# Lead of the attention: three score tiles, merged exponentials, last keys by quarters, and an order that knows of tiling changes

## The chip, the cores and the metric

The kernel runs on one core of one Trainium2 chip. The metric is the device time of one execution in microseconds (us). The kernel before takes 1019.68 us, the median of three runs (1018.27 to 1021.52).

## The reference

Three blocks follow each other, all in float32, on 4 batches, 12 heads, 448 positions and heads of 64. B, S and DM below are 4, 448 and 768.

```python
# attention with a soft cap
scores = matmul(q, k.T) / sqrt(64)
scores = cap * tanh(scores / cap)
attn = exp(scores - max(scores)); attn = attn / (sum(attn) + 1e-9)
x = matmul(attn, v)                      # B, H, S, 64 -> x: B, S, DM = 12 * 64
# normalised FFN with a residual
xn = (x - mean(x)) / sqrt(var(x) + 1e-6) * g_ln
x = x + relu(xn @ w_ch1) @ w_ch2         # DM -> 4 DM -> DM
# gated MLP over positions
h = relu(x @ w_in); u, v = h[:512], h[512:]
v = (v - mean(v)) / sqrt(var(v) + 1e-6)
out = (u * (w_spatial @ v + b_spatial)) @ w_out
```

## The kernel before

**Layout.** Features stand on the 128 partitions and the 448 positions in the free dimension. Two heads are worked on together: they fill 64 partitions each, so that a product of one head takes half of the TensorE array and the other head's product runs beside it. The code calls the first head of such a pair `i`; this document calls the pair a unit. Batches 0 and 1 make units 0, 2, ... 22, batches 2 and 3 make 24 to 46. Attention products of the first two batches are float32, each of which the trace shows as two instructions; FFN products are float32 values split into a high and a low part of type float32r, three products for one.

**A unit of attention.** The 448 keys are three chunks of 128 and a last one of 64. `emit_s` computes the scores of a chunk transposed (keys on partitions) into a two-bank PSUM tile (`twos`, there are two), one bank a head: array shape 64 rows x 128 columns. ScalarE then applies Tanh (`expo`, from PSUM into an `es` tile) and Exp in place. The max isn't subtracted, since the cap bounds the scores. `emit_st` computes the last 64 keys of two units at once, with 64x64 quarters of the array, into two single banks; ScalarE works on each bank by itself (`hs` tiles). `emit_v` makes the products with the values (128 rows x 64 columns, two heads side by side). For the last keys it contracts over all 128 partitions, and half of the value tile is zero (memset at the start). VectorE adds up the three chunks' exponentials and then the last keys' (`add`, 64 partitions a head); a product with ones turns that into the sums over keys (128x32 for two units, 128x64 where a unit is `alone`: the last four heads of a batch). Reciprocals come back through DRAM (`invert`) or, for unit 22, from VectorE; `emit_n` multiplies and `x_done` adds the result to the sum over features from which the mean of a batch is made (`ln_mean`, `feature_sum`: two float32r products with ones). `ln_center` subtracts the mean and splits the result into `xn`.

**Stages.** `main` builds the program in this order: the lead (`attend` for units 0 to 22, with `ln_mean` and `ln_center` of batch 0 at place 16.2 of 24 and those of batch 1 after the last unit, and four FFN weight tiles through `make` from place 1.0 on), then `h_units`, the first FFN product of batches 0 and 1 (a unit of it is 18 products of 128x128, 3 for each of 6 feature blocks), with the attention of batches 2 and 3 between, and then second FFN products (`y_seven`), the gated MLP and a second pass for batches 2 and 3.

**The order.** Nothing above is the order on the chip. `Program` records every operation with a cost; `edges` finds what depends on what, `order` gives each a due time from the sum of TensorE costs before it, and `plan` plays the engines and at each step takes, on a free engine, the ready operation that is due first and for which buffers are free (`pick`, `room`). On TensorE a `group` is taken as one, with an added constant (`switch`) where the writer expected a change of array shape. TensorE may run ahead of its due times by 28 us (`AHEAD`). `Stage` opens a set of SBUF buffers when an earlier set has been used up. Operations in `either` go to VectorE or ScalarE, whichever plays out better.

Of the kernel before, what the change touches and what calls it, by code (L numbers as in the profile page):

```python
# [38 lines left out]
ST = 0.12  # L39

# [3 lines left out]
FIRST = 2, 7, 2, 10, 2, 2  # L44


AHEAD = 28
SLACK = 0.35
# [66 lines left out]
class Stage:  # L115


    def __init__(self, prog, tc, name, after=(), side=None):
        self.side = side
        self.tc, self.name, self.after, self.then, self.pools = tc, name, after, [], []  # L120
        self.open = not after
        self.left = 0
        self.pool = None
        for a in after:
            a.then.append(self)
        prog.stages.append(self)

    def begin(self):
        self.pool = self.tc.tile_pool(name=self.name, bufs=1, side=self.side)
        pool = self.pool.__enter__()  # L130
        for p in self.pools:
            for t in p.tiles:
                t.tile = pool.tile(t.shape, t.dt, name=t.name)
# [12 lines left out]
class Slots:  # L146


    def __init__(self, name, tiles, proto=None, stage=None):
        self.name, self.size = name, len(tiles)  # L150
# [65 lines left out]
class Program:  # L216
# [6 lines left out]
    def __init__(self, nc):  # L223
# [3 lines left out]
        self.at = {}  # L227
        self.stages = []
# [16 lines left out]
    def add(self, engine, cost, latency, call, writes, reads):  # L245
        o = self.open
        if o is None:
# [13 lines left out]
    def group(self, switch=0.0):  # L261


        self.switch = switch
# [3 lines left out]
        o[0][0][1] += self.switch  # L268
# [85 lines left out]
    def plan(self, due):  # L354
# [38 lines left out]

        def pick(e):

# [3 lines left out]
            found = None  # L399
            while q and found is None:  # L400
                d, i, k = heapq.heappop(q)
                if taken[i]:
                    continue
                if d > reach():
# [12 lines left out]
                if not room(i):  # L417
                    skipped.append((d, i, k))
                    continue
                found = i, k  # L420
            for x in skipped:
                heapq.heappush(q, x)
# [6 lines left out]
        while True:  # L429
            for e in ready:  # L430
# [13 lines left out]
                if e == "PE":  # L444
                    spent += cost
                free[e] = now + cost
# [24 lines left out]
            else:  # L471
                for b in bufs[x]:
                    b.left -= 1
                    if not b.left:
                        b.pool.give(b)
                        if b.pool.stage is not None and not b.pool.stage.left:
                            for s in b.pool.stage.then:
                                if not s.open and all(not a.left for a in s.after):
                                    s.open = True
                                    out.append((s, None))  # L480
                                    for p in s.pools:
                                        p.changes += 1
# [16 lines left out]
class Recorder:  # L499
# [3 lines left out]
    def __getattr__(self, method):  # L503
# [5 lines left out]
        def record(*args, **kw):  # L509
# [30 lines left out]
            self.program.add(self.name, cost, latency, call, [out], ins)  # L540
# [5 lines left out]
def attn_ffn_gmlp_kernel(  # L546
# [37 lines left out]
    def slots(name, n, shape, dt, pool=const):  # L584
# [6 lines left out]
            ("wh", [128, 2, DM], F32R), ("small", [128, 80], F32)), COUNTS))  # L591

    shapes = {"rb": ([128, 2, DH], F32R), "w6": ([128, DM, 2], I32), "es": ([128, 2, S], F32),
# [5 lines left out]
    def staged(stage, kind, n, name=None):  # L599
# [5 lines left out]
    mid = Stage(prog, tc, "mid", (one,))  # L605
# [6 lines left out]
    w6, es, qks, hx, wc, w4 = (  # L612
        staged(one, kind, n, name) for (kind, name), n in zip(
            (("w6", "w6"), ("es", "es"), ("qk", "qk"), ("acc", "hx"), ("wq", "wc"), ("w4", "w4")), FIRST))
# [16 lines left out]
    ones64 = const.tile([128, 64], F32, name="ones64")  # L631
    ones32 = const.tile([128, 2], F32, name="ones32")
    onesr = const.tile([128, 128], F32R, name="onesr")
# [3 lines left out]
    mhalf = const.tile([128, 64], F32, name="mhalf")  # L637
# [3 lines left out]
    banks = slots("bank", 4, [128, 512], F32, psum)  # L641
    twos = slots("two", 2, [128, 2, 512], F32, psum)

    def f(t):
        return t.bitcast(F32)

# [47 lines left out]
    def value(kind, j, home=None, pool=wr):  # L694
# [8 lines left out]
        else:  # L703
# [5 lines left out]
            if home is None:  # L709
                A.activation(out=t, in_=hi.bitcast(F32), func=ACTF.Prelu, scale=REBASE, alpha=-(2.0 ** 32))  # L710
            else:
                with prog.either():
                    for e in (V, A):
                        if e is A:
                            A.activation(out=t, in_=hi.bitcast(F32), func=ACTF.Copy, scale=REBASE)
                        else:
                            V.tensor_scalar(out=t, in0=hi.bitcast(F32), scalar1=REBASE, scalar2=None, op0=ALU.mult)
# [4 lines left out]
            else:  # L722
                V.tensor_scalar(out=ti, in0=ti, scalar1=3, scalar2=None, op0=ALU.logical_shift_left)
                if home is not None:
# [1086 lines left out]
```

## Time and profile before

| | us |
|---|---|
| median of 3 runs | 1019.68 (1018.27 to 1021.52) |
| span of the profiled execution | 1016.5 |
| busy: PE | 1002.0 (99%) |
| busy: VectorE (DVE) | 856.2 (84%) |
| busy: ScalarE (ACT) | 565.4 (56%) |
| chain that ended last | PE 75%, DMA 14%, DVE 5%, ACT 4% |

The profile page gives one execution by its span, from the first to the last instruction; it shows no other time of that execution, and the times of the runs are measured separately. Ends of matmuls are modelled, so a busy PE may still be waiting inside; the distance between the starts of its instructions tells more. All operations are recorded through one helper, so every row names the same line (L538); the tiles' names tell the operations apart: `two<-qk` are scores, `bank<-qk` last scores, `bank<-es,vt` and `bank<-hs,vt` values and last values, `bank<-es,ones` the sums, `bank<-rs,wh` and `bank<-rs,rs` FFN products, `bank<-wh,onesr` products of `feature_sum`.

### The profile page before, as it was taken

The numbers are of one execution on the slowest core, as the hardware profiler recorded it, in microseconds if no ns is written. First come the engines' busy times: TensorE is split into PE (matmuls) and PEld (weight loads), VectorE is DVE, ScalarE is ACT, GpSimd is POOL, SyncE is SP. The second block draws the span as 40 slices with busy tenths as digits, with TensorE's granted clock in tenths as the row PEclk, the third lists the DMA queues.
The fourth block names the chain that finished last, engine by engine and source line by source line (L and its number), as shares of the span: only waits on it lengthen the run. The fifth ranks groups of instructions, "written<-read, shape, count | busy, mean of one in ns | idle before, by whom it ended". The sixth has DMA issues, their size and how long they took to land.

```text
span 1016.5 us, 14927 instructions
## 1 busy us (share of the span) xinstructions
PE 1002.0 (99%) x5056; PEld 825.9 (81%) x5056; DVE 856.2 (84%) x1476; ACT 565.4 (56%) x897; POOL 24.3 (2%) x21
## 2 busy tenths in 40 slices
PE   7999999999999999999999999999999999999998
PEld 2332787787778889999889899999999999998887
DVE  6989998878888779989889989877788777778986
ACT  7999776776667344545566245544465322214553
POOL 0000110000000000000001110000000000000000
PEclk9999999999999999999999999999999999999999
DMA  8454779999999999999684233565799986602402
GB/s 261 154 139 144 256 279 360 359 337 369 338 370 363 358 341 403 409 329 375 244 259 144 50 133 117 165 203 194 236 336 395 337 267 222 192 21 71 132 17 109
DMA packets 132048, 248.71 MB, mean 245 GB/s; under 512 B 21970, under 2 KB 93828, under 8 KB 131972
## 3 DMA queue, kind: packets, MB, share of 16 engines
q1 hardware_dynamic: 131972, 247.76, 70.9%
q8 instruction: 40, 0.66, 0.3%
q14 instruction: 36, 0.29, 0.1%
HBM read 167.70 MB, written 80.01 MB: 244 GB/s over the span
## 4 chain that ended last, share of the span: by engine, by line
PE 75%; DMA 14%; DVE 5%; ACT 4%; issue 1%; SPq 1%; DVEq 0%; ACTq 0%
PE bank L538 50%; PE two L538 25%; DMA w<-in_w_dram 5%; DMA kept_w<-wc 3%; DMA hs<-inv 2%; ACT es L538 2%; DMA qk<-in_qk_dram 1%; DMA h<-hx 1%; ACT hs L538 1%; DVE x L538 1%; DMA inv<-rc 1%; SPq L538 1%; DVE rs L538 1%; DVE wh L538 1%; DVE small L538 1%
## 5 line engine op out<-in xcount | busy, mean ns | idle before, releaser
L538 PE MATMUL bank<-rs,wh 128*128 128x448 f32 x1704 | 357.1, 363 | 2.5 <-ACT hs L538 2.2
L538 PEld LDWEIGHTS bank<-rs,wh 128*128 128x128 f32 x1704 | 318.2, 187 | 29.9 <-ACT hs L538 4.4
L538 DVE TENSOR_TENSOR rs<-hs,rs 128x448 fp32r<-128x448 f32 x159 | 94.8, 619 | 3.7 <-ACT rs L538 3.1
L538 PE MATMUL two<-rs,wh 128*128 128x448 f32 x414 | 92.7, 362 | 0.0
L538 ACT ACTIVATE rs<-hs 128x448 fp32r<-128x448 f32 x118 | 64.5, 569 | 36.8 <-DMA hs<-h 27.6
L538 PEld LDWEIGHTS two<-rs,wh 128*128 128x128 f32 x414 | 77.6, 188 | 5.2
L538 ACT ACTIVATE es<-es,capt 128x896 f32<-128x896 f32 x72 | 73.5, 1062 | 0.0
L538 DVE TENSOR_TENSOR wh<-wr,wh 128x768 fp32r<-128x768 f32 (+2 forms) x72 | 62.0, 863 | 5.3 <-ACT wh L538 5.1
L538 ACT ACTIVATE es<-two,qsc 128x896 f32<-128x896 f32 x62 | 61.1, 1023 | 7.4 <-PE two L538 7.4
L538 PE MATMUL bank<-es,vt 128*64 128x448 f32 x288 | 62.1, 552 | 0.0
L538 ACT ACTIVATE wh<-wr 128x768 fp32r<-128x768 f32 (+2 forms) x57 | 44.1, 773 | 27.0 <-DVE wr L538 12.6
L538 DVE TENSOR_TENSOR es<-es,es 128x896 f32<-128x896 f32 x48 | 51.9, 1082 | 2.3 <-ACT es L538 1.8
L538 ACT ACTIVATE hs<-bank 128x448 f32<-128x448 f32 x60 | 32.3, 540 | 37.8 <-PE bank L538 31.2
L538 PEld LDWEIGHTS bank<-es,vt 128*64 128x64 f32 x288 | 17.4, 136 | 36.6 <-issue 27.1
L538 PE MATMUL two<-qk 64*128 64x448 f32 x168 | 40.7, 591 | 5.7 <-DMA qk<-in_qk_dram 4.2
L538 ACT ACTIVATE wc<-w 128x512 f32<-128x512 f32 x36 | 24.1, 673 | 29.4 <-DMA kept_w<-wc 14.6
L538 ACT ACTIVATE rs<-x 128x448 fp32r<-128x448 f32 x34 | 19.0, 573 | 37.7 <-DVE x L538 36.5
L538 PEld LDWEIGHTS two<-qk 64*128 64x128 f32 x168 | 14.3, 192 | 29.6 <-ACT es L538 15.0
L538 PE MATMUL two<-wh,rs 128*128 128x512 f32 x144 | 35.8, 395 | 0.1
L538 ACT ACTIVATE wh<-wqm 128x768 fp32r<-128x768 f32 x20 | 16.9, 844 | 32.0 <-PE bank L538 20.0
L538 PE MATMUL bank<-rx,whb 128*128 128x448 f32 x144 | 32.7, 362 | 0.0
L538 PE MATMUL two<-rx,whb 128*128 128x448 f32 x144 | 32.7, 362 | 0.0
(232 smaller groups left out, 1873.2 us busy)
## 6 DMA issues: line engine op xcount, KB each, us to landing
hs<-h SPq DMA_DIRECT2D x168, 224.0 KB, 5.8
h<-hx SPq DMA_DIRECT2D x84, 224.0 KB, 4.9
w<-in_w_dram SPq DMA_DIRECT2D x24, 768.0 KB, 6.8
w<-in_w_dram SPq DMA_DIRECT2D x36, 512.0 KB, 6.2
wqm<-kept_w SPq DMA_DIRECT2D x30, 384.0 KB, 6.2
qk<-in_qk_dram SPq DMA_DIRECT2D x24, 448.0 KB, 5.0
h<-hs SPq DMA_DIRECT2D x48, 224.0 KB, 4.0
kept_w<-wr SPq DMA_DIRECT2D x24, 384.0 KB, 7.5
```

The costliest lines, as they stand in the source:

```text
L538: fn(*(put(a) for a in args), **{k: put(a) for k, a in kw.items()})
```

## The change

In the lead alone (units 0 to 22):

- `lead_s`: a unit takes three score tiles at once, the two of `twos` and a third (`t3`) that stands in the place of banks 2 and 3. Each chunk has a Tanh; one Exp covers the three chunks (2688 elements), but for unit 0, which has one for each. Stage `third` holds `t3`; when it is used up, `others` opens banks 2 and 3 in its place. Until then there are two single banks.
- `lead_st`: last scores of two units go to one two-bank tile, with one Tanh and one Exp.
- `lead_v`: the last keys' values of two units are products of 64x64 quarters (`last_products`); no half of the value tile is zeroed any more. The last keys are no longer added on VectorE: the sums are made of several products, one with ones for the added exponentials and one with `sel`, which has ones in the unit's half and zeros in the other, for the last keys. In units 14, 18, 20 and 22 (`DIRECT`) the third chunk's exponentials are not added but have a product of their own. Only units 20 and 22 are `alone`.
- `ln_mean` of batch 1 (`MEANS`) multiplies the six feature blocks with ones in float32 (`direct_sum`) instead of adding them on VectorE. It and `ln_center` of batch 1 stand after the first FFN unit of batch 0. Those of batch 0 stand at place 15.2.
- The four weight tiles are made from place 3.1 on, and by the route of all others (a Prelu on ScalarE, two VectorE operations).
- SBUF: `pre` holds two three-chunk exponential tiles (`e3`) and six `es` tiles for the lead; when it is used up, `ffn` opens seven `es` and nine `hx` (ten before) in its place. `mixed_h` needs one tile fewer.

In the whole kernel: `group` has no constant; the planner keeps the array shape of each product (`modes`), adds 0.17 us where it changes, and `pick` on TensorE prefers, among operations due within 3 us of the first, one of the present shape.

```diff
 FAST = 22,
-FIRST = 2, 7, 2, 10, 2, 2
+MAKE = 3.1
+LN_AT = 3.2
+SECOND = 0
+DIRECT = 14, 18, 20, 22
+MEANS = 1,
+FIRST = 2, 2, 2, 2
+REST = 7, 9
+LEAD = 2, 6
+SWITCH = 0.17
+NEAR = 3.0
...
             while q and found is None:
                 d, i, k = heapq.heappop(q)
...
+                if first is not None and d > first[0] + NEAR:
+                    skipped.append((d, i, k))
+                    break
...
+                if e == "PE" and self.modes[i][0] != mode:
+                    first = first or (d, i, k)
+                    skipped.append((d, i, k))
+                    continue
                 found = i, k
+            if found is None and first is not None:
+                found = first[1:]
...
+    def lead_s(i):
+        t = raws[i]
+        e = e3.get()
+        scs = [p.get()[:, :, 0:S] for p in (twos, twos, t3)]
+        for c, sc in enumerate(scs):
+            with prog.group():
+                for half in range(2):
+                    r = slice(64 * half, 64 * half + 64)
+                    T.matmul(out=sc[:, half], lhsT=t[r, S + 128 * c:S + 128 * c + 128], rhs=t[r, 0:S],
+                             start=True, stop=True)
+        for c, sc in enumerate(scs):
+            A.activation(out=e[:, c], in_=sc, func=ACTF.Tanh, scale=qsc)
+            if i == 0:
+                A.activation(out=e[:, c], in_=e[:, c], func=ACTF.Exp, scale=capt)
+        if i:
+            A.activation(out=e, in_=e, func=ACTF.Exp, scale=capt)
+        st[i] = e
+
+    def lead_v(i):
+        b, h = heads[i]
+        u, E, et = raws["v", i], st.pop(i), st.pop(("t", i))
+        s = es0.get()
+        add(s, E[:, 0], E[:, 1])
+        parts = [s]
+        if i in DIRECT:
+            parts.append(E[:, 2])
+        else:
+            add(s, s, E[:, 2])
+        x = xts[b][h // 2]
+        todo.append((i, parts, x, et))
+        now = todo[:] if i // 2 % 2 or alone(i) else []
+        ps = tails[i] if i in tails else banks.get()[:, 0:S]
+        for ns in [range(3)] if i else [[n] for n in range(3)]:
+            with prog.group():
+                for n in ns:
+                    for half in range(2):
+                        r = slice(64 * half, 64 * half + 64)
+                        T.matmul(out=ps[r], lhsT=u[:, values(i, n, half)], rhs=E[:, n, half],
+                                 start=n == 0 and i not in tails, stop=n == 2 and i in tails)
+        if i // 2 % 2 == 0:
+            with prog.group():
+                last_products(i, ps, et)
+        cp(x, ps, (V, A))
+        pr = banks.get()[:, 0:S] if now else None
+        width = 64 if len(now) == 1 else 32
+        if now:
+            with prog.group():
+                most = max(len(a) for _, a, _, _ in now)
+                for m in range(most + 1):
+                    for n, (j, a, _, e) in enumerate(now):
+                        if m < most and m >= len(a):
+                            continue
+                        for half in range(2):
+                            q = (2 * n + half) * width
+                            T.matmul(out=pr[q:q + width], lhsT=sel[:, j // 2 % 2, 0:width] if m == most else ones128[:, 0:width],
+                                     rhs=(e if m == most else a[m])[:, half], start=m == 0, stop=m == most)
...
+    def direct_sum(ps, xs):
+        for k, x in enumerate(xs):
+            with prog.group():
+                T.matmul(out=ps, lhsT=ones128, rhs=x, start=k == 0, stop=k == KD - 1)
...
     def alone(i):
-        return i < 2 * H and i % H >= H - 4
+        return 2 * H - 4 <= i < 2 * H
...
                     mine[b, j] = h_unit(b, w[j])
+                    if j0 == 0 and (b, j) == (0, SECOND):
+                        ln_mean(1)
+                        ln_center(1)
...
             if i < 2 * H:
-
-                stages += [(2.05, emit_v, i, (0, 1)), (2.15, emit_v, i, (2, 3))]
+                stages = [(0.0, lead_s, i), (2.05, lead_v, i)] + stages[2:]
...
-        lead = attend(0, 2 * H, 1.0) + [(x, fn, (b,)) for x, b in ((H + 4.2, 0), (2 * H + 2.25, 1)) for fn in (ln_mean, ln_center)]
-        lead += [(1.0 + j * H / EARLY, make, ("w1", j)) for j in range(EARLY)]
+        lead = attend(0, 2 * H, 1.0) + [(H + LN_AT, fn, (0,)) for fn in (ln_mean, ln_center)]
+        lead += [(MAKE + j * H / EARLY, make, ("w1", j)) for j in range(EARLY)]
```

## Rows read from the trace of the kernel before

**Rows 1.** Stretches: us, busy us (instructions) of PE, PEld, DVE, ACT, POOL; PEclk, DMA, GB/s.
```profile
18.00:45.00 27.00, 27.00 (x144) 8.56 (x144) 26.32 (x41) 27.00 (x34) 0.00 (x0) 1.00 0.59 186
...
90.00:101.00 11.00, 9.74 (x41) 2.81 (x41) 10.16 (x20) 11.00 (x17) 0.00 (x0) 1.00 0.35 97
...
123.00:340.00 217.00, 215.00 (x1194) 167.92 (x1195) 182.51 (x295) 150.22 (x216) 8.43 (x2) 1.00 0.98 345
```

**Rows 2.** Timeline of PE, one period: start us, us, engine, operation [idle before].
```profile
25.84 1.77 PE L538 MATMUL two<-qk 64*128 64x448 f32 x8
27.55 1.72 PE L538 MATMUL bank<-es,vt 128*64 128x448 f32 x8
29.20 1.02 PE L538 MATMUL two<-qk 64*128 64x448 f32 x4
30.15 0.97 PE L538 MATMUL bank<-es,vt 128*64 128x448 f32 x4
...
38.71 0.96 PE L538 MATMUL bank<-es,ones 128*32 128x448 f32 x8
39.59 1.77 PE L538 MATMUL two<-qk 64*128 64x448 f32 x8
```

**Rows 3.** Timeline of all engines, the start.
```profile
1.65 0.42 SPq L538 DMA_DIRECT2D w<-in_w_dram  x1
...
4.24 3.35 PE L538 MATMUL two<-qk 64*128 64x448 f32 x8 [4.24 <-DMA qk<-in_qk_dram]
...
9.56 0.97 PE L538 MATMUL bank<-qk 64*64 64x448 f32 x4 [0.33 <-DMA qk<-in_qk_dram]
```

**Rows 4.** Timeline of PE, the end of the lead.
```profile
74.90 1.77 PE L538 MATMUL two<-qk 64*128 64x448 f32 x8
...
90.13 2.00 PE L538 MATMUL bank<-qk 64*64 64x448 f32 x4
...
101.00 3.91 PE L538 MATMUL bank<-rs,rs 128*128 128x448 f32 x18
```

**Rows 5.** Groups of PE by shape, 4 to 101 us: xcount | busy us, mean ns.
```profile
L538 PE MATMUL bank<-hs,vt 128*64 128x448 f32 x48 | 11.7, 541 | 0.0
...
L538 PE MATMUL bank<-es,ones 128*32 128x448 f32 x32 | 4.4, 551 | 0.0
L538 PE MATMUL bank<-es,ones 128*64 128x448 f32 x16 | 4.2, 539 | 0.0
```

**Rows 6.** Timeline of PE, first FFN units and the mean of batch 1.
```profile
112.01 0.90 PE L538 MATMUL bank<-wh,onesr 128*128 128x448 f32 x2
112.74 3.77 PE L538 MATMUL bank<-rs,wh 128*128 128x448 f32 x18
...
122.82 3.98 PE L538 MATMUL bank<-rs,rs 128*128 128x448 f32 x18
```

**Rows 7.** Timeline of PE, an FFN unit between two attention runs.
```profile
258.23 3.88 PE L538 MATMUL bank<-rs,wh 128*128 128x448 f32 x18
```

**Rows 8.** Timeline of ACT in the same period.
```profile
23.70 1.03 ACT L538 ACTIVATE es<-two,qsc 128x896 f32<-128x896 f32 x1
24.59 0.67 ACT L538 ACTIVATE hs<-bank,qsc 128x448 f32<-128x448 f32 x1
25.11 2.01 ACT L538 ACTIVATE es<-es,capt 128x896 f32<-128x896 f32 x2
26.97 0.67 ACT L538 ACTIVATE hs<-bank,qsc 128x448 f32<-128x448 f32 x1
27.49 0.71 ACT L538 ACTIVATE hs<-hs,capt 128x448 f32<-128x448 f32 x1
28.05 1.05 ACT L538 ACTIVATE es<-two,qsc 128x896 f32<-128x896 f32 x1
```

**Rows 9.** Groups of DVE by shape, 4 to 101 us.
```profile
L538 DVE TENSOR_TENSOR es<-es,hs 64x448 f32<-64x448 f32 x24 | 13.9, 616 | 0.3
```

**Rows 10.** Waits, 10 to 100 us: who waits for whom, us in total, times, longest.
```profile
PEld two L538 <- ACT es L538: 15.0, 24, 1.6
```

More of the change, by code (lines that the diff above doesn't have):

```diff
@@ L146, with __init__ @@
 class Slots:
-    def __init__(self, name, tiles, proto=None, stage=None):
-        self.name, self.size = name, len(tiles)
+    def __init__(self, name, tiles, proto=None, stage=None, late=()):
+        self.name, self.size, self.late = name, len(tiles) + len(late), list(late)
         self.proto = tiles[0] if proto is None else proto
@@ L243, in region, with add @@
         return name, p0, p0 + ap.ap[0][1], c0, c1
-    def add(self, engine, cost, latency, call, writes, reads):
+    def add(self, engine, cost, latency, call, writes, reads, mode=None):
         o = self.open
+        if mode is not None:
+            seen = self.modes.setdefault(len(self.ops), [])
+            if seen and seen[-1] != mode:
+                o[0][0][1] += SWITCH
+            seen.append(mode)
         if o is None:
@@ L481, in plan @@
                                     for p in s.pools:
+                                        p.changes += 1
+                                    for p in s.more:
+                                        p.idle.extend(p.late)
                                         p.changes += 1
@@ L636, in attn_ffn_gmlp_kernel @@
     g_t = const.tile([128, KD], F32, name="g_t")
-    mhalf = const.tile([128, 64], F32, name="mhalf")
+    mhalf = const.tile([128, 8], F32, name="mhalf")
     tok_t = [[const.tile([128, NCT], F32, name=f"{n}_t{i}") for n in ("var", "rstd")] for i in range(2)]
     rst = [const.tile([128, S], F32, name=f"rstd{i}") for i in range(2)]
-    banks = slots("bank", 4, [128, 512], F32, psum)
+    banks = Slots("bank", [psum.tile([128, 512], F32, name=f"bank{i}") for i in range(2)],
+                  late=[Later(f"bank{i}", [128, 512], F32) for i in range(2, 4)])
+    others.more.append(banks)
     twos = slots("two", 2, [128, 2, 512], F32, psum)
+    t3 = third.slots("t3", 1, [128, 2, 512], F32, twos.proto)
     def f(t):
         return t.bitcast(F32)
+    ones128 = f(onesr)
     def sub(o, a, b, engines=None):
@@ L1002, in ln_center @@
     def ln_center(b):
-        mean, sq = means.pop(b), hs.get()
+        mean, sq = means.pop(b), None if b in SQUARES else hs.get()
         xn[b] = []
@@ L1513, in product @@
                                  skip_group_check=True)
[L1515 removed]
+        h11, h22, h12, h21, t1, t2, t4 = (p.get() for p in (h2, hs, hs, h2, h2, hs, hs))
         def snap(o, ps):
@@ L1749, in attn_ffn_gmlp_kernel @@
     one.begin()
+    pre.begin()
+    third.begin()
     with tc.manual_schedule():
@@ L1753, in attn_ffn_gmlp_kernel @@
         nc.scalar.activation(out=t[:], in_=t[:], func=ACTF.Tanh)
-        for p, u in zip((slice(64, 128), slice(0, 64)), vts):
-            nc.gpsimd.memset(u.tiles[0].tile[p, 384:512], 0.0)
         prog.issue()
```

137 lines of the change are left out of this document (88 added, 49 removed).

## The prediction

> **What bounds the kernel now.** First the table of stretches [rows 1]. The granted clock stays at 1.00, its 2.4 GHz level. From 123 to 340 us TensorE is busy 215.00 of 217 us: that is full, and nothing but fewer or shorter products helps there. The first 101 us, the attention of the first two batches, which I call the lead, read differently: from 18 to 45 us three engines are full together (PE and ACT 27.00 of 27, DVE 26.32), and from 90 to 101 PE drops to 9.74 of 11 while ACT has 11.00. A busy PE proves little, so the second view is PE's timeline, read by the distance of the starts.
>
> [Rows 2] hold one period of the lead, two units (a unit is two heads), from 25.84 to 39.59, 13.75 us. Two score chunks of two heads take 27.55 - 25.84 = 1.71 us, one alone 30.15 - 29.20 = 0.95: a set of tiled products, the ones that share the array, costs about 0.75, and the remaining 0.2 comes once for a run of one shape. The period has 16 sets (6 of scores, 1 of last scores, 6 of values, 2 of last values, 1 of sums) and 10 changes of shape; 16 x 0.75 = 12.0, and 13.75 - 12.0 = 1.75 makes 0.175 a change. So here PE is not waiting at all; it pays for sets and changes. The timeline from 4.24 to 101.00 has 60 changes (its first and last PE rows are in [rows 3, 4]).
>
> PE does lose time at both ends. At the start [rows 3] the first two chunks take 3.35 us instead of 1.77, and then PE waits to 9.56 for the second load of q and k, which was issued behind a weight's (1.65). Up to 13.07 it has done 6 sets and 4 changes, 5.2 us of work in 8.8: 3.6 lost. At the end [rows 4] 90.13 to 101.00 holds 9 sets and 6 changes, 7.8 us in 10.9: 3.1 lost. From 74.90 to 90.13 the same count gives 17 sets and 11 changes, 14.7 of 15.2 us: 0.5 more.
>
> **The change, part by part.**
>
> *Sets in the lead.* Last values had a set per unit, 48 instructions or 12 sets [rows 5]; now two units share one: -6. Sums had 4 sets for pairs and 4 for single units (32 and 16 instructions). Now the five pairs take 2 sets, 3 where one of them keeps the third exponential as its own product (14 and 18), and units 20 and 22 take 3 each: 2+2+2+3+3+3+3 = 18, which is +10. Scores do not change. Net +4 x 0.75 = +3.0 us, at full price because PE is the queue that is full.
>
> *Mean of batch 1.* Six f32 products on the whole array replace two that take 112.74 - 112.01 = 0.73 us [rows 6]. No f32 product of 128x128 stands in the trace. Below, it could cost what a product of the FFN does, 3.77/18 = 0.21 us, then the part costs +0.5; above, a tiled set fills the same array with the same columns, 0.75. I take the set, since it is the same type and length: 4.5 - 0.7 = +3.8. The work runs after the lead, where PE goes from unit to unit without a wait, and the vector adds it saves were hidden anyway.
>
> *Changes of shape.* With three score tiles the three chunks of a unit are one run, not two, and the order prefers the present shape within 3 us. A period then goes scores, values, last values with last scores, scores, values, sums: 6 changes, 7 if the two 64-row runs do not meet, instead of 10. Over six periods that is 18 to 24 fewer; I take 20 x 0.175 = -3.5. In the FFN part the runs are joined already: only now and then does one unit of 18 products stand between two attention runs [rows 7], two changes for each. Three such places are 1.0 us; I take -0.5, and bound it at -1.0 and, as another order can also part runs, +1.5.
>
> *ACT.* Tanh of a chunk starts another after 0.89, an Exp after 0.93 (26.97 - 25.11 halved), the half tiles after 0.52 and 0.56 [rows 8]. For a period 6 x 1.82 + 2 x 1.08 = 13.1 us: level with PE's 13.75, since copies come on top. Merged, the Exp of 2688 elements costs 0.93 plus 1792 x (0.93 - 0.56)/448 = 2.41, and last scores become one pair of 1.82: 6 x 0.89 + 2 x 2.41 + 1.82 = 12.0. So ACT gets 1.1 us a period. That is worth nothing by itself while PE is the bound; it is what lets PE's losses go. ACT also gains work: four weight tiles get their first step on ACT, about 0.8 each by an Exp's size, 3 us in all.
>
> *DVE.* The 24 last-key adds go, 13.9 us busy [rows 9], with four wide adds and those of batch 1's mean. All beside PE, priced at nothing: in the period PE has no wait that DVE could end. DVE then has room for the normalisation of batch 0, whose products can fill PE at the lead's end.
>
> *Both ends.* At the start the weights move behind two units (MAKE), so q and k no longer queue behind them, the third chunk has its own tile, and unit 0's exponentials and values go chunk by chunk. The slow first products stay, and ACT needs 0.89 + 0.93 a chunk before the first value: of 3.6 lost I take back 1.8 (bounds 0 and 3.0). At the end, units of batch 0 are ready earlier and no last-key add stands before the sums: of 3.1 + 0.5 I take back 3.4 (bounds 1.5 and 3.6).
>
> *What is late next.* The ACT chain before each values run (three Tanh, one long Exp, 5.1 us), two banks instead of four until the third tile is gone, and the new stage order: the exponential tiles of batch 2 and the FFN's outputs cannot open until the lead's last sums are done. Batch 1 now starts its mean after a unit of batch 0, with three units (11 us) and the attention of batch 2 as cover; before, 21.8 us lay between the lead's end (101.00) and batch 1's first product at 122.82, without a wait [rows 6]. I put +0.5 for all of this, bounded by 0 and rival two.
>
> **The sum.** 3.0 + 3.8 - 3.5 - 0.5 - 1.8 - 3.4 + 0.5 = -1.9 us. The profiled span of 1016.5 becomes 1014.6. The page gives no time of that execution but its span; the median of the timed runs, 1019.68, lies 3.2 above it, and with the same 3.2 the forecast is 1017.8.
>
> **A rule weighed.** Four column tiles of a sums set cost the same 0.75 as two row tiles: 39.59 - 38.71 is 0.88 with its change [rows 2]. The Trainium skill (TensorE: Matmul & The Clock Gate, Measured speedup vs the span model) measures 2.38 times for three column tiles, not 3. By that share a sums set would be 0.75 x 3/2.38 = 0.95, an estimate from that page, and the ten new ones 2 us dearer; the row disagrees, and the sum keeps 0.75.
>
> **Rivals.**
> *One, faster (0.26):* the losses go entirely. Every bound at its good end, 3.0 back at the start, 3.6 at the end, 24 changes fewer, 1.0 in the FFN, nothing new late: 3.0 + 3.8 - 4.2 - 3.0 - 3.6 - 1.0 = -5.0, 1014.7. With the mean's products at 0.21 it would be 3.2 less, 1011.5. For it: ACT and DVE both get off the limit. Against: ACT must still feed the first units.
>
> *Two, slower (0.17):* the merged Exp makes PE stand in each unit. Values of a unit wait for one 2.41 us instruction where before the first two chunks' values could begin without the third's Exp, and the next scores need tiles that ACT is slow to empty. Already now weight loads of scores wait for ACT 24 times, 15.0 us in all, 0.62 each [rows 10], though hidden. If 0.62 a unit came through, 12 x 0.62 = 7.4, less the 0.5 counted: +5.0, 1024.7. From (1.9 + 0.5)/12 = 0.2 us a unit on there is no gain, and from 0.46 the kernel is slower by 0.3%. Against: ACT's 12.0 of PE's 13.2 us a period leaves room, if scores run a unit ahead. The Trainium skill (Perfetto Trace Analysis, Optimizing Scalar/DVE Operations) says the same: when ACT is not full but makes bubbles on another engine, break its instructions up. The trace of before has ACT full, the case in which that page groups instead; after the change it would no longer be.
>
> *Three, the order does not do what it says (0.10):* tiles come free one at a time, so shapes still alternate: 54 changes, -1.1 instead of -3.5, FFN 0: +1.0, 1020.7.
>
> **Chances.** My forecast 0.47, by itself 1015 to 1020.5. A difference under 0.3%, 3.1 us, cannot be told from none. Faster: rival one's 0.26 and 0.14 of the forecast, 0.40. Same: 0.33 of the forecast and 0.08 of three, 0.41. Slower: rival two 0.17 and 0.02 of three, 0.19. The range runs from rival one's lower end, 1011.5, to just under rival two's price, 1024.5.
>
> **What would show it.** Right: the sums' sets in the lead 18, changes near 40, a period near 13.2 us, no wait from 85 us to the first FFN product, the FFN's first product near 95 us (92 where batch 2's first scores come after it), six products of 0.75 for the mean. Wrong: PE waiting for the long Exp in each unit (rival two), 50 or more changes (three), a gap before batch 1's first product, mean products at 0.2, or a difference that arises after 340 us, where I expect none.

## The result, and the profile after

The changed kernel takes 1024.27 us (median of 10 runs, 1020.97 to 1030.45), the kernel before 1018.66 beside it: ratio 1.0056, 95% interval 1.0036 to 1.0077. It is slower; the forecast was 1.9 us faster. The profiled span went from 1016.5 to 1022.4 us, +5.9.

To see where, I cut PE's timeline of both kernels at the same point of the work and count from start to start. From each stretch I take the products (0.75 us a set of the lead or an f32 product on the whole array, 0.20 a product of the FFN) and 0.18 for each change of shape; what is left is the rest: waits and half-filled sets.

```
stretch (before / after ends)          elapsed          products        changes   rest
first PE to batch 1's first FFN unit   118.58 -> 120.62  96.98 -> 103.30  65 -> 55  9.90 -> 7.41
to the end of the attention (337/339)  214.32 -> 214.73  the same         50 -> 50  2.76 -> 3.17
to 563 / 567                           225.51 -> 227.65  the same          1 ->  1  3.41 -> 5.55
to 970 / 976                           407.36 -> 408.66  the same          8 ->  8  3.42 -> 4.73
the end                                 42.58 ->  42.80  the same          7 ->  7  1.33 -> 1.55
```

So 1.9 us are lost in the lead and its seam to the FFN (2.04, less 0.18 of earlier start), and 4.0 afterwards, where the work is the same. First the lead: PE's timeline of the changed kernel (start, us, engine, line, operation, tiles and shape, count, and in brackets the idle time before and who ended it).

```profile
4.06 3.36 PE L568 MATMUL two<-qk 64*128 64x448 f32 x8 [4.06 <-DMA qk<-in_qk_dram]
...
15.92 0.98 PE L568 MATMUL bank<-es,vt 64*64 64x448 f32 x8 [0.30 <-ACT es L568]
...
19.51 1.02 PE L568 MATMUL two<-qk 64*128 64x448 f32 x4
21.93 2.48 PE L568 MATMUL bank<-e,vt 128*64 128x448 f32 x12 [1.40 <-ACT e L568]
24.34 0.96 PE L568 MATMUL bank<-es,onesr 128*32 128x448 f32 x8
25.11 0.93 PE L568 MATMUL bank<-es,sel 128*32 128x448 f32 x8
25.98 0.98 PE L568 MATMUL two<-qk 64*64 64x448 f32 x8
...
34.96 2.48 PE L568 MATMUL bank<-e,vt 128*64 128x448 f32 x12 [0.32 <-ACT e L568]
...
53.63 1.77 PE L568 MATMUL two<-qk 64*128 64x448 f32 x8
...
90.07 3.92 PE L568 MATMUL bank<-rs,rs 128*128 128x448 f32 x18
...
97.72 0.92 PE L568 MATMUL bank<-es,sel 128*64 128x448 f32 x4
98.58 1.02 PE L568 MATMUL bank<-x,onesr 128*128 128x448 f32 x2
99.08 0.92 PE L568 MATMUL bank<-wh,onesr 128*128 128x448 f32 x2
99.84 0.91 PE L568 MATMUL bank<-x,onesr 128*128 128x448 f32 x2
100.69 1.77 PE L568 MATMUL two<-qk 64*128 64x448 f32 x8
...
106.85 0.91 PE L568 MATMUL bank<-x,onesr 128*128 128x448 f32 x2
107.70 1.02 PE L568 MATMUL two<-qk 64*128 64x448 f32 x4
108.65 1.02 PE L568 MATMUL bank<-x,onesr 128*128 128x448 f32 x2
109.60 0.98 PE L568 MATMUL bank<-qk 64*64 64x448 f32 x8
...
124.68 3.98 PE L568 MATMUL bank<-rs,rs 128*128 128x448 f32 x18
```

The end of the lead [rows 4] is repaired: from 82 to 98.58 nothing is lost, and an FFN unit of batch 0 runs inside it at 90.07. The start is not: instead of the load [rows 3], PE waits 1.40 at 21.93 for the long Exp of its second unit. Behind the lead the mean's products (`bank<-x,onesr`) come one by one: some stand beside other products on the whole array, one (108.65) alone between two tiled runs.

Next the part after 340 us. At about 371 us the second weight's second product begins, with a tile `whm` made from a load `wqm<-kept_w`. That load goes to memory in which converted weights (`wc`) and FFN outputs (`hx`) have waited for their stores, so it can't be issued before the last of these has landed. The text below calls this point the gate. The timeline there, of PE and then of SP, first of the kernel before, then of the changed one:

```profile
371.01 0.67 PE L538 MATMUL two<-rs,whm 128*128 128x448 f32 x2 [0.70 <-ACT whm L538]
372.00 2.27 PE L538 MATMUL two<-rs,whm 128*128 128x448 f32 x10 [0.32 <-DVE whm L538]
```

```profile
355.38 0.55 SPq L538 DMA_DIRECT2D kept_w<-wc  x1
...
357.64 1.61 SPq L538 DMA_DIRECT2D h<-hx  x3
...
363.92 1.32 SPq L538 DMA_DIRECT2D wqm<-kept_w  x3
```

```profile
373.71 0.68 PE L568 MATMUL two<-rs,whm 128*128 128x448 f32 x2 [1.61 <-ACT whm L568]
375.16 3.85 PE L568 MATMUL two<-rs,whm 128*128 128x448 f32 x10 [0.77 <-DVE whm L568]
```

```profile
363.88 0.54 SPq L568 DMA_DIRECT2D kept_w<-wc  x1
...
368.43 0.32 SPq L568 DMA_DIRECT2D wqm<-kept_w  x1
```

The last converted weight is stored 8.5 us later, the load issued 4.5 later, and PE, which comes 1.8 later, waits 2.4 instead of 1.0. In the kernel before, the last store ahead of the load is one of `hx`, not of `wc`, and SP doesn't wait right before the load. In the changed kernel it does, for the landing of a `wc` store (SP's waits from 367 to 368.6 us: who waits for whom, us, times, longest):

```profile
SPq L568 <- DMA kept_w<-wc: 1.3, 1, 1.3
```

Then ten products take 3.85 us instead of 2.27. The table of stretches of the changed kernel shows the clock there (busy time and count of PE, PEld, DVE, ACT, POOL; granted clock, DMA share, GB/s):

```profile
371.00:375.00 4.00, 1.77 (x8) 0.97 (x6) 2.14 (x4) 0.86 (x2) 0.00 (x0) 1.00 0.86 254
375.00:379.00 4.00, 3.84 (x11) 3.48 (x12) 3.71 (x7) 2.54 (x3) 0.00 (x0) 0.57 1.01 349
```

After 1.77 busy us of 4 the granted clock averages 0.57, near its lower level of 1.2 GHz. The same table from 100 us on, of the kernel before and of the changed one, shows how busy the DMA engines are ahead of the load:

```profile
100.00:140.00 40.00, 39.94 (x199) 30.81 (x196) 37.16 (x63) 30.45 (x48) 7.92 (x1) 1.00 0.70 226
140.00:340.00 200.00, 198.00 (x1112) 153.51 (x1109) 165.58 (x267) 136.79 (x196) 1.02 (x1) 1.00 1.01 361
```

```profile
100.00:140.00 40.00, 40.00 (x193) 28.57 (x193) 33.45 (x58) 27.07 (x40) 1.02 (x1) 1.00 0.65 203
140.00:340.00 200.00, 198.47 (x1109) 152.22 (x1108) 165.54 (x266) 135.35 (x192) 1.82 (x1) 1.00 1.01 355
```

PE is not alone near its limit: from 140 us on the 16 DMA engines have a share of 1.01 in either kernel, by that figure no idle time. I had read [rows 1] for the engines and left out their last two columns.

### The profile page after: what moved, and what is told of

It reads as the page before. It is cut to its first block, busy times and chain, and to the rows that moved or that the text cites. A ratio compares the mean times of both kernels' runs of the same rounds, so it can differ in the third digit from the quotient of the medians.

```text
span 1022.4 us, 15003 instructions
## 1 busy us (share of the span) xinstructions
PE 1006.7 (98%) x5130; PEld 830.9 (81%) x5130; DVE 840.0 (82%) x1447; ACT 554.0 (54%) x850; POOL 17.8 (2%) x21
## 4 chain that ended last, share of the span: by engine, by line
PE 78%; DMA 11%; DVE 4%; ACT 3%; SPq 1%; issue 1%; DVEq 0%; ACTq 0%
PE bank L568 51%; PE two L568 26%; DMA kept_w<-wr 2%; ACT e L568 2%; DMA w<-in_w_dram 2%; SPq L568 1%; DMA hs<-inv 1%; DMA kept_w<-wc 1%; DMA qk<-in_qk_dram 1%; DVE small L568 1%; DMA x<-hs 1%; DMA h<-hx 1%; DVE rs L568 1%; ACT es L568 1%; PE t L568 1%
## 5 line engine op out<-in xcount | busy, mean ns | idle before, releaser
L568 ACT ACTIVATE rs<-hs 128x448 fp32r<-128x448 f32 x126 | 68.1, 569 | 31.4 <-DMA hs<-h 25.7
L568 ACT ACTIVATE wh<-wr 128x768 fp32r<-128x768 f32 (+2 forms) x53 | 40.8, 770 | 30.5 <-DVE wr L568 14.2
L568 ACT ACTIVATE hs<-bank 128x448 f32<-128x448 f32 x56 | 30.1, 540 | 33.0 <-PE bank L568 29.1
L568 ACT ACTIVATE es<-es,capt 128x896 f32<-128x896 f32 x42 | 42.3, 1048 | 0.0
L568 PE MATMUL two<-qk 64*128 64x448 f32 (+1 forms) x168 | 36.0, 593 | 4.1 <-DMA qk<-in_qk_dram 4.1
L568 PE MATMUL bank<-es,vt 128*64 128x448 f32 (+1 forms) x192 | 35.6, 551 | 0.3 <-ACT es L568 0.3
L568 ACT ACTIVATE es<-two,qsc 128x896 f32<-128x896 f32 x32 | 31.9, 1011 | 3.4 <-PE two L568 3.4
L568 PEld LDWEIGHTS two<-qk 64*128 64x128 f32 (+1 forms) x168 | 12.4, 180 | 24.8 <-issue 8.7
L568 PEld LDWEIGHTS two<-wh,rs 128*128 128x128 f32 x144 | 26.9, 187 | 6.7 <-DVE rs L568 0.2
L568 PE MATMUL bank<-e,vt 128*64 128x448 f32 x144 | 29.9, 548 | 1.9 <-ACT e L568 1.7
```

Source lines behind the costliest of these rows:

```text
L568: fn(*(put(a) for a in args), **{k: put(a) for k, a in kw.items()})
```

## Experiments

Each ratio is to the kernel before, timed beside it. The other figures, in us, are those of one profiled execution each, whose time lies up to 2.8 us off the median (e15):

```
                  ratio  [95%]            first part  last wc store  PE at the gate  next product
before            -                         118.58       355.4          369.95        371.01
after             1.0056 [1.0036, 1.0077]   120.62       363.9          371.72        373.71
e1 no means       1.0064 [1.0040, 1.0088]   115.43       362.0          365.23        371.88
e2 no preference  1.0236 [1.0211, 1.0261]   121.03       378.8          384.59        388.71
e3 ahead early    1.0109 [1.0081, 1.0136]   120.20       365.8          371.56        378.88
e4 old lead       1.0097 [1.0068, 1.0126]   126.02       367.6          376.27        377.79
e5 three Exps     1.0177 [1.0153, 1.0201]   123.77       371.9          372.89        382.29
e8                1.0135 [1.0113, 1.0158]   124.01       322.9          376.28        381.11
e9                1.0168 [1.0139, 1.0198]   128.18       321.3          378.31        381.35
e10               1.0089 [1.0065, 1.0112]   129.11       315.7          378.28        378.48
e11 more DMA      1.0039 [1.0021, 1.0058]   119.44       356.2          370.69        371.58
e12 fewer stores  1.0036 [1.0021, 1.0050]   119.83       336.0          370.65        370.85
e13 and no means  0.9974 [0.9960, 0.9989]   114.91       333.7          365.46        365.67
e14 before, fewer 1.0039 [1.0023, 1.0056]   121.55       336.3          376.14        376.34
e15 start early   1.0028 [1.0009, 1.0047]   115.36       360.0          368.36        370.31
e16 make early    1.0076 [1.0047, 1.0106]   116.31       365.4          368.44        375.39
e17 both early    1.0029 [1.0012, 1.0046]   118.97       358.2          368.60        368.80
e18 before, 27    1.0059 [1.0035, 1.0083]   119.97       357.8          368.80        369.93
e19 after, 27     1.0100 [1.0078, 1.0122]   121.19       365.9          374.15        377.41
e20 both, 27      1.0112 [1.0075, 1.0149]   116.11       354.1          373.73        374.33
```

"First part" is the first stretch of the table above; "PE at the gate" is the start of the last product before `two<-rs,whm`. The last `wc` store isn't always the last store ahead of the load: in the kernel before, in e8 to e14, e18 and e20 it is an `hx` store.

**e1: the mean's products out of the changed kernel.**
```diff
-MEANS = 1,
+MEANS = ()
```


> The changed kernel with batch 1's mean made as before (added on VectorE, two float32r products). Theory A (TensorE is full after the lead, so six f32 products cost their price): 4.5 - 0.7 = 3.8 us less than the changed kernel, and the changes of array shape that these products make between attention runs (7 from 101 to 120 us, 2 before) go as well, some 1 us: 1019 to 1020. Rival (the products filled a wait for batch 1's normalisation): the wait shows instead, 0 to 1 us less, 1023 to 1024.


The first part is 5.2 us shorter: 4.1 of products, 3 changes, and some waits. That is theory A's price, yet the time is that of the changed kernel, as the rival said, but not for the rival's reason: the wait is at the gate. PE's timeline there, then SP's, and the clock behind it:
```profile
361.83 3.77 PE L568 MATMUL bank<-rs,wh 128*128 128x448 f32 x18
371.88 5.01 PE L568 MATMUL two<-rs,whm 128*128 128x448 f32 x12 [6.28 <-ACT whm L568]
```
```profile
363.88 2.42 SPq L568 DMA_DIRECT2D hs<-inv  x4
366.40 2.94 SPq L568 DMA_DIRECT2D wqm<-kept_w  x5
```
```profile
372.00:376.00 4.00, 4.00 (x10) 3.12 (x11) 3.40 (x5) 2.53 (x3) 0.00 (x0) 0.50 1.02 380
```
PE arrives 6.5 us earlier and waits 6.28 us for the same load; then twelve products take 5.01 us, which take some 2.4 at full clock. Here the load is issued 4.4 us behind the last `wc` store, straight after four other loads (`hs<-inv`) and without a wait of SP for a `wc` or `hx` store, so its place in SP's queue comes in, and that store alone needn't be what holds it.

**e2: no preference for the present shape; e4: the kernel before with that order (its core alone shown).**
```diff
-SWITCH = 0.17
-NEAR = 3.0
+SWITCH = 0.0
+NEAR = -1.0
```


> The changed kernel with an order that does not know of tiling changes (no cost of a change, no preference for the present shape). If the preference is what took the changes of shape from 65 to 55 up to 123 us, they rise again by 5 to 10 and the first 125 us get 1 to 2 us longer. If three score tiles alone did it, the count stays within 3. After 340 us: if the later losses (3.7 us) come from the order of the whole kernel, they change; if from scatter, they differ without relation to the edit.


```diff
+                if e == "PE" and self.modes[i][0] != mode:
+                    first = first or (d, i, k)
+                    skipped.append((d, i, k))
+                    continue
```


> The kernel before with the new order alone (cost and preference of array shapes). Theory A (the late losses come from the lead's new parts and the stages): like before in the later part, and in the first 123 us 5 to 15 changes fewer, 1 to 2.5 us: 1016 to 1018. Rival (the new order itself moves the weight conversions and costs the time after 337 us): a wait over 2 us near 370 us and 2 to 4 us more than before, 1020 to 1022.


Without the preference the changed kernel has 58 changes in the first part, with it 55; the old lead with it has 66, one more than before, and its first part is 7.4 us longer, 6.5 of it waits. So the preference is worth about three changes here, and the rest of the ten comes with the lead's new tiles and sums. e4, 0.97% slower, lies above both of its theories: the new order saves the old lead no change and costs it waits. e2's large loss is not in the lead, and most of it comes one FFN unit before the gate, where PE waits for a tile of the first weight; then 18 products take 6.49 us instead of some 3.6:
```profile
378.47 6.49 PE L568 MATMUL bank<-rs,wh 128*128 128x448 f32 x18 [12.30 <-ACT wh L568]
388.71 5.05 PE L568 MATMUL two<-rs,whm 128*128 128x448 f32 x12 [3.75 <-DMA wqm<-kept_w]
```

**e3: second weight's conversions closer together.**
```diff
-AFTER = 0.05, 0.9, 0.93
+AFTER = 0.05, 0.86, 0.93
```


> The changed kernel with the conversions of the second FFN weights asked for somewhat earlier (the last at 0.86 instead of 0.90 of the first FFN product). Theory A (the wait of 2.7 us near 372 us and the 3.4 us of half clock behind it come from the last conversions, stored 8.5 us later than before, which hold back the stage of the next weights): the last store is issued before 358 us, the wait falls under 1.5 us, the clock stays full, 2 to 3 us less: 1021 to 1022. Rival (scatter of one execution, or DMA bandwidth): no change, within 1 us of 1024.


A miss: the last store comes 1.9 us later, not earlier, and the time, 1028.88, lies above both theories. The load is issued at 373.33, 7.5 us behind that store; just before, SP waits 1.4 us for the landing of another store (`inv<-rc`). An earlier due time didn't make the conversions earlier here.

**e8, e9, e10: six of these conversions moved into the lead, of the changed kernel without the mean's products, of the changed kernel, and of the kernel before.**
```diff
+        lead += [(8.0 + 2.5 * j, ahead, rows[j]) for j in range(FROM)]
```


> The changed kernel with batch 1's mean made as before and the first 6 of the 36 conversions of second FFN weights in the lead (from unit place 8 on), the rest 6 places earlier. Theory A (from 140 to 430 us the DMA engines are full, so the second FFN product starts when some 109 MB have been moved, whatever TensorE gained): 6 x 0.77 MB leave the full stretch, 4.6 MB / 0.343 MB/us = 13 us of it; the wait of 6.7 us near 366 and the 6.8 us of half clock go, 6 to 9 us less than with the mean alone: 1015 to 1018, under the kernel before. Rival (a latency in the order of SP's queue, not bandwidth): the wait stays over 4 us, 1021 to 1025.

> The changed kernel with the same 6 conversions in the lead, batch 1's mean by f32 products as changed. Theory A: without the wait near 372 the mean's price shows in the time, 4 to 5 us more than the run without it: 1019 to 1022. Rival (queue order): 1022 to 1025, as the changed kernel.

> The kernel before with the same 6 conversions in the lead. Theory A: only 1.3 us of wait near 370 can go, and ACT and DVE, which are full in its lead, get 6 conversions more (about 2 us each over both): 1018 to 1024, not faster. Rival (the lead of before has room as well): 1015 to 1017.


Misses, all three: 1034.66, 1037.18 and 1029.05 us, above both theories of each. The lead gets 7.6 to 10.5 us longer. The `wc` stores end some 40 us earlier, and the gate doesn't open earlier, for now the `hx` stores are last (367 to 372). From 140 to 373 us the DMA share is only 0.94 to 0.97, so theory A's price, bytes over a full rate, doesn't hold; in e8 PE still waits 4.46 us, as the rival (the order of SP's queue) said. How much of that is the longer lead these runs don't tell.

**e11: nine stores of 224 KB more in the kernel before.**
```diff
+            todo += [(total * (0.30 + 0.04 * j), spill, (j,)) for j in range(9)]
```


> The kernel before with 9 stores more (229 KB each, 2.06 MB, a tile to scratch memory) between 0.30 and 0.62 of the first FFN product. Theory A (DMA engines full from 140 to 430 us): the first product of the second FFN's next weights, at 371.0 before, starts 2.06/0.343 = 6 us later, and the half clock that a long wait brings adds some 2 us: 1024 to 1028. Rival (DMA has slack, latency decides): within 1.5 us of before.


It is 0.4% slower, but not at the gate: the order put these stores at 380 to 444 us, behind it, so the run doesn't test the theory. PE waits for later weights:
```profile
423.63 0.68 PE L538 MATMUL bank<-rs,wh 128*128 128x448 f32 x2 [0.78 <-ACT wh L538]
...
428.83 0.67 PE L538 MATMUL bank<-rs,wh 128*128 128x448 f32 x2 [0.73 <-ACT wh L538]
```

**e12, e13, e14: 24 stores less before the gate, in the changed kernel, in e1, and in the kernel before.**
```diff
+            if n in (5, 6) and not last_pass[0]:
+                hidden[n, i] = hidden[1, i]
+                continue
```


> Changed kernel; 24 of the hidden stores of the first pass (the products n = 5 and 6) are left out, some 5.5 MB less for the DMA queues to move between 140 and 350 us, and the later loads read product 1's tile instead, so the output isn't the reference's. Theory A: the 3.7 us that the changed kernel loses after 337 us come from a weight load that is ready too late because the DMA engines are full up to it; then the long PE wait before the first product of the second half (372 us) and the half granted clock behind it go, and the time falls 3 to 5 us below the changed kernel, to about 1020. Theory B: the wait has to do with when the conversions of the weights are issued by the other engines, not with bytes; then the wait stays and the time is within 1 us of the changed kernel.

> As the run before, and besides the six f32 products of batch 1's mean are taken out (the mean is summed by VectorE as in the kernel before). Theory A: the 5 us by which this lead ends earlier are no longer eaten by the wait for the weight load, so the time is 4 to 6 us below the run with fewer stores alone. Theory B: the same time as that run, since the gate is set by something that an earlier TensorE doesn't move.

> Kernel before with the same 24 hidden stores left out. Theory A: the kernel before waits little at that gate (about 1 us), so the time falls by only 1 to 2 us, to about 1017; the changed kernel with fewer stores is then 2 us slower than this one (the length of its lead), the one without the mean's products 3 us faster. Theory B: it falls as much as the changed kernel does, and the difference between the two kernels stays 5.6 us.


PE at the gate in e12, then in e13:
```profile
361.65 9.36 PE L568 MATMUL bank<-rs,wh 128*128 128x448 f32 x46
370.85 2.56 PE L568 MATMUL two<-rs,whm 128*128 128x448 f32 x12
```
```profile
361.66 4.17 PE L568 MATMUL bank<-rs,wh 128*128 128x448 f32 x20
365.67 2.73 PE L568 MATMUL two<-rs,whm 128*128 128x448 f32 x12
```
The wait and the low clock are gone, and the stretch to 563 takes 225.28 and 224.69 us. In e12 the profiled span falls by 2.7 us against the changed kernel's (2.4 of it in this stretch), the median by 0.2% only, less than the 3 us expected. In e13 the earlier PE now stays earlier: 0.62% below e12, 0.26% below the kernel before. That is the only run which beats it, and it leaves stores out, so it is no version to use. e14 came out wrong by both theories: slower than the kernel before. No wait is left at its gate; it loses 3.0 us in the lead and 3.7 in the attention, with waits of 1.2 and 1.9 us between attention runs (188, 329). The edit also makes the planner draw another order, here a worse one, and I can't price the stores from it. The same holds against e12 and e13, though there both orders lose the wait.

**e5: an Exp for each chunk, as rival two would have it.**
```diff
-        if i:
-            A.activation(out=e, in_=e, func=ACTF.Exp, scale=capt)
+            A.activation(out=e[:, c], in_=e[:, c], func=ACTF.Exp, scale=capt)
```


> Changed kernel with one Exp for each chunk of keys in the lead instead of one over the three. Theory A (the merged Exp makes TensorE stand little): 12 x 2 more ScalarE instructions, each with its own fixed part, in a stretch where ScalarE is not the bound; within 1 us of the changed kernel, the wait of 1.75 us at 20 us shorter. Theory B (the merged Exp makes TensorE wait in every period): the lead ends 3 us or more earlier.


Neither theory: 12 us slower than the changed kernel. PE's timeline, and then one stretch of this kernel and of the changed one:
```profile
44.16 1.08 PE L568 MATMUL bank<-es,vt 64*64 64x448 f32 x8
46.33 1.77 PE L568 MATMUL two<-qk 64*128 64x448 f32 x8 [1.09 <-DMA qk<-in_qk_dram]
...
382.29 1.12 PE L568 MATMUL two<-rs,whm 128*128 128x448 f32 x2 [9.04 <-ACT whm L568]
```
```profile
26.00:82.00 56.00, 53.96 (x308) 17.96 (x310) 39.61 (x59) 53.51 (x61) 0.00 (x0) 1.00 0.54 162
```
```profile
26.00:82.00 56.00, 55.55 (x338) 19.21 (x334) 41.80 (x63) 54.05 (x47) 0.00 (x0) 1.00 0.59 177
```
The wait of 1.40 at 21.93 is gone, and to 38 us this kernel is 0.8 us ahead (last scores start at 38.30 instead of 39.11). Then it falls behind: ACT is 96% busy in both, and PE does 308 products in the stretch instead of 338. I put that down to ACT, which has 22 instructions more in the lead (unit 0 had its three before); the profile names a load of q and k for the longest wait (46.33), and the run doesn't part the two. The first part is 3.2 us longer, the first converted weight is stored later (105.9 us instead of 96.1), and at the gate the wait is 9.04 us.

**e15, e16, e17, all without the mean's products: second weight's conversions begin earlier; first weight's again at their old place; both.**
```diff
-AFTER = 0.05, 0.9, 0.93
+AFTER = 0.0, 0.9, 0.93
-MAKE = 3.1
+MAKE = 1.0
```


> Changed kernel without the mean's f32 products (1024.2 by itself), and the conversions of the second weight begin at the first FFN unit instead of a twentieth of the way through. Theory A (the weight load near 370 us is late since the DMA engines, full from 140 us on, start on the conversions too late): the load comes 3 us or more earlier, TensorE's 6.45 us wait before it falls to 3 or less, the time to 1020 or less. Theory B (only the number of bytes counts, which is unchanged, and the half idle engines before 140 us can't take more because ACT and DVE are busy): same time within 1.5 us, or a longer lead.

> Changed kernel without the mean's f32 products, and the first weight's conversions due at 1.0 units of the lead instead of 3.1. Theory A (the change pushed them back, and everything behind them on DMA, ACT and DVE with them): TensorE waits up to 2 us at the start for the q and k loads again, but the second weight's conversions come 3 to 5 us earlier and the time falls 3 us, to 1021. Theory B (the conversions of the first weight have room in the lead): start 1 to 2 us longer and the time 1025 or more.

> Both of the two runs before together. Theory A: the gains add, TensorE's 5 us of the lead survive, and the time is 1016 to 1018, below the kernel before. Theory B: no less than the better of the two.


e15 goes the way of theory A, but short of its price: from 100 to 140 us the DMA share is 0.73 instead of e1's 0.65, the load is issued 2.2 us earlier, PE's stand at the gate falls from 6.65 to 1.95 us (start to start), and the time to 1021.29. Of these 4.7 us only 1.6 are an earlier product behind the gate; in the other 3.1 PE comes later, having lost them in the attention. e16 goes as theory B said. In e17 PE no longer waits at the gate (368.60 to 368.80), but its first part is 3.6 us longer than e15's, and its time, 1021.95, is no better.

**e18, e19, e20: another look-ahead of the planner, in the kernel before, the changed kernel and e17.**
```diff
-AHEAD = 28
+AHEAD = 27
```


> Kernel before with the planner's look-ahead at 27 products instead of 28: the same work in another drawn order. If the kernel before had just drawn a good order for the late part, this one loses 1 to 5 us after 125 us (waits of TensorE between attention runs and at the weight load near 370 us). If the order alone is worth nothing, the time stays within 1 us of the kernel before, and the 4 us that the change loses late have their cause in the change itself.

> Changed kernel with the look-ahead at 27 products instead of 28, the same work in another order. Theory A (the late 4 us are the draw of an order, and the kernel before had a good one): this kernel moves too, by 2 us or more either way, and where the first product behind the load near 370 us starts follows TensorE's arrival and the load; it stands near the kernel before's own re-drawn 1024.3, that is 1020 to 1028. Theory B (the change itself makes that load late): within 1 us of the changed kernel, 1023.3 to 1025.3.

> The run with both kinds of conversions early and no mean's f32 products (1022.0), with the look-ahead at 27. Theory A: the order draws another time, anywhere from 1017 to 1027. Theory B: within 1 us of 1022.0.


`AHEAD` is counted in us of planned TensorE work, not in products as the expectations have it. All three get slower, by 0.4 to 0.8%; e19, at 1029.14, and e20, at 1028.69, lie above both theories' ranges. PE at the gate in e18 and e19:
```profile
369.93 0.68 PE L538 MATMUL two<-rs,whm 128*128 128x448 f32 x2 [0.77 <-ACT whm L538]
```
```profile
377.41 0.68 PE L568 MATMUL two<-rs,whm 128*128 128x448 f32 x2 [2.89 <-ACT whm L568]
```
An order alone is worth as much as the whole change, so a difference of this size in one edit proves little. But the pair repeats: with either look-ahead the changed kernel is 0.4 to 0.6% behind its partner, its last `wc` store 8.1 or 8.5 us later, and its wait at the gate over 2 us against 1. That speaks for a loss that belongs to the change and not to the draw; two draws don't prove it.

## Why the prediction was wrong

It failed in two places, by nearly equal parts: 3.8 of 7.8 us up to batch 1's first FFN unit, 4.0 behind it.

```
term                                   forecast   measured
sets and the mean's products             +6.8       +6.3
changes in the lead                      -3.5       -2.9  (60 -> 44)
changes behind it                        -0.5       +1.1  (5 -> 11)
start                                    -1.8       +0.7, less 0.2 of earlier start
end of the lead                          -3.4       -4.1
what is late next                        +0.5       +1.2 in the middle, -0.3 behind the lead
up to the FFN's batch 1                  -1.9       +1.9
after that                                0         +4.0
```

The whole lies just inside the stated range and beside rival two's price of 1024.7 us. That is luck: rival two's waits for the long Exp come to 1.7 us here, and the rest has other causes.

**Right:** the price of a full-array f32 product: the set's 0.75, not the FFN's 0.21 (98.58 to 100.69 holds two of them, two products of 0.20 and a change: 2.1 us; and e1, without six, has a first part 5.2 us shorter); the 18 sums' sets (two of them half-filled); the lead's end. There the reading of before was off by three changes: 90.13 to 101.00 holds 4 and not 6, 74.90 to 90.13 ten and not 11, so that 4.1 us were lost and not 3.6, and these 4.1 came back. Nearly right: the first FFN unit at 90 us instead of 95 and 44 changes instead of 40. Not so the period: it stayed at 13.8 us ((53.63 - 25.98)/2) and didn't fall to 13.2, with 7.5 changes instead of 6 or 7 and 0.5 us of waits and half-filled sets. Two sums' sets start 0.77 apart (24.34 and 25.11), so the row decides against the 0.95 that I had estimated from the Trainium skill (TensorE: Matmul & The Clock Gate, Measured speedup vs the span model).

**Wrong, the start.** I gave back half of the 3.6 us lost up to 13.07. By 25.98 the changed kernel has a rest of 5.2 us, by 25.84 the kernel before 4.5 [rows 2, 3]. The wait for the load went, and the chain that I had named under "what is late next" (three Tanh, one long Exp) came in its place: 1.40 at 21.93 and 0.32 at 34.96. That is rival two's mechanism, in the first units only. To part every Exp again is no cure, as e5 shows: by the trace ACT is still full in the lead (54.05 of 56 us), so the condition under which the Trainium skill advises it (Perfetto Trace Analysis, Optimizing Scalar/DVE Operations) isn't met here.

**Wrong, the changes behind the lead.** I priced the mean's products as if they stood in a row and brought no change. They come one at a time, as their values do: e1 without them has 8 changes from 97 us on, the changed kernel 11, the kernel before 5. The part cost 5.2 us instead of 3.8, for vector work that was hidden.

**Wrong, "no difference after 340 us".** I took the PE-bound stretch to mean that later PE work only shifts. The gate at 371 us is set by loads and stores on the DMA queues, which don't come earlier when PE does. e1 shows it from one side (an earlier PE gains nothing), e12 and e13 from the other (fewer stores, no wait, the gain stays). Of the 4.0 us, 2.1 arise there; 1.3 arise in the stretch to 976, 0.92 of it in one wait at 766, which no run explains.

**Open:** why the stores are behind. The runs don't part two causes, the limit of the DMA engines and the order of SP's queue, in which a load waits its turn (e1, e3, e8). By the GB/s and lengths of the stretches, the changed kernel moved 0.9 MB less from 100 to 140 us (203 against 226 GB/s), but from 0 to 140 us both move 188 GB/s, so at 140 it isn't behind. From 140 to 340, where the share is 1.01 in both, it moves 1.2 MB less; that the same share moves fewer bytes (355 against 361 GB/s) I can't explain.

## What to carry to other kernels

When a stretch is full on one engine, read its DMA share too: where that is also 1.0, ask which later point waits for a load or a store, for a gain ahead may end there: e1's 5.2 us were lost at the gate and in the low clock behind it. Don't move hidden vector work to a full TensorE, and price its f32 products as whole sets with the changes of shape that they bring (three for six products here). Where a planner draws the order, repeat the pair with one setting changed that leaves the work alone: here that setting was worth 0.4 to 0.8%, as much as the change, and a single pair would have told little.

## What the runs showed of the hardware

A wait of PE near 370 us can be paid twice. In the changed kernel (1.77 of 4 us busy) and in e1 (6.28 us idle) the granted clock fell to its 1.2 GHz level behind it, and in e1 the 12 products after it took 5.01 us instead of 2.4; in the kernel before, after 0.70 and 0.32 us, and in e18, after 0.77, it stayed at 2.4 GHz. The timed runs agree: their mean granted clock was 0.996 in e1, 0.998 in the changed kernel and 1.000 in e13, which has no such wait; of the changed kernel's ten, the three at 1.000 took 1020.97 to 1022.61 us, the seven below it 1023.73 to 1030.45.
